# Turning x for the MLP's pairs 4 to 7 on VectorE instead of TensorE, in a fused transformer block

## The chip, the cores and the metric

The kernel runs on one core of a Trainium2 chip. A core has five engines, each with its own queue of instructions that it works through in order: TensorE (PE in the profile; PEld are its weight loads), VectorE (DVE), ScalarE (ACT), GpSimd (POOL) and SyncE (SP, which here only starts transfers). Engines wait for each other by semaphores. Transfers between the chip's DRAM and the on-chip memory (SBUF) run on 16 DMA engines, started from SP's, ACT's or POOL's queue. Matrix products land in PSUM, which ACT and DVE read.

The metric is the device time of one execution, in microseconds (us). The kernel before takes 766.53 us, the median of three runs (766.48 to 767.01).

## The reference

All is float32, for S = 2048 tokens, D = 640 features, 32 heads of 20, and F = 1728 hidden features:

```
mod = (silu(c) @ w_mod) in six rows of 640: sa, ca, ga, sb, cb, gb
h = layernorm(x) * (1 + ca) + sa
x = x + ga * linear_attention(h)              # softmax feature maps, then @ wo
h = layernorm(x) * (1 + cb) + sb              # layernorm over the 640 features of a token
r = relu(h @ w1 + b1)
x = x + gb * ((r * r) @ w2 + b2)
```

The change lies in the second layernorm and in how its result is brought to the MLP's first product.

## The kernel before

The attention half takes the first half of the time; its result for token tile t (128 tokens) lies in DRAM as `A1[t]`. The MLP then goes over eight **pairs** j = 0 to 7 of two token tiles, 256 tokens each. Float32 products are made of three products of rounded parts (high times high, high times low, low times high), so each operand exists as a high and a low part.

For a pair j the MLP runs seven **rounds** n = 0 to 6, and each round has two **steps**: step 2n and step 2n + 1, so that a pair has steps 0 to 13. In step s TensorE makes `up(j, s)`: 128 hidden features for the 256 tokens, 15 matmuls over the five blocks d of the features (10 in step 13, whose tile is half). ACT takes it from PSUM with bias and relu into `ft` (`ACTIVATE ft<-up`), DVE squares it there. After the second step of a round ACT copies the high parts into `ra`, DVE makes the low parts of it (`ra<-ft,ra`) and four sums (`ft<-ft` of 128 elements) that the next step splits into `rs` in the same way. From `ra` TensorE makes the first half of the down product, `down(0)`, in the following even step, behind `up`; from `rs` the second half, `down(1)`, in the following odd step. For pairs from 2 on, four of the operands of `down` come through rings of four buffers, fetched by POOL's queue (`t_fetch`), and a seven-product scheme replaces eight products.

The MLP reads the normalised input turned: features on the partitions, tokens along the row, in five blocks d = 0 to 4 (`H2[j]`, named `h` in the profile). While pair j is in work, the input of pair j + 1 is made ready in small pieces; `layer(j + 1, s)` puts a piece behind step s. The table `LN_AT` says at which step each piece stands (`LN_AT0`, `LN_AT1` and `LN_AT2` do it for pairs 1 to 3). The pieces are:

- `load`: `xm` gets `A1`'s two tiles, `xx` the block's input x (both token-major: tokens on the partitions).
- `add`: DVE adds `xx` to `xm`; SP stores the sum as `X1[j]`, which is read again later as the residual (`xr<-x`).
- `ln`: six pieces, two each of a sum, a sum of squares and a normalising pass over the 640 features (all ACT, with small work on POOL in between for mean, variance and the power -0.5).
- the entries 8, 10 and 12, which name blocks d: `t2` turns these blocks with TensorE (`t_in`, four transposes for two blocks, two for one), and `t_out` applies scale and shift by feature on ACT, makes the high part on ACT and the low part on DVE.

The result of pair j - 1 is finished in rounds 0 to 2 of pair j (`first_combos`, `end`, `gate`, `finish`), and `finish` also stores it to `out` through SP's queue.

The order within each engine's queue is that in which the code is written; from pair 2 on SP's queue is included.

Of the kernel before, what the change touches and what calls it, by code (L numbers as in the profile page):

```python
# [8 lines left out]
F32 = mybir.dt.float32  # L9
# [6 lines left out]
P = 128  # L16
S = 2048
D = 640
# [17 lines left out]
KEPT = NT - POSTPONED  # L36
W2_AT = 48
PLAIN = 2
DIRECT = 2
LAST = 3  # L40
W_AT = (
# [10 lines left out]
def kernel(  # L52
# [47 lines left out]
    tiny.tile([P, 144], F32, name="fill2")  # L100
# [16 lines left out]
    def row(tag, name):  # L117
        return (pc if tag in ("s3", "s4") else mem).tile([P, D], F32, tag=tag, name=name, bufs=BUFS[tag])
# [13 lines left out]
    def small(shape, tag, name, bufs=2):  # L132
        return (pc if tag in ("mx", "sk", "dn", "dd") else tiny).tile(shape, F32, tag=tag, name=name, bufs=bufs)
# [4 lines left out]
    def tp(name):  # L138
        return psA.tile([P, 512], F32, tag="tp", name=name)
# [160 lines left out]
    def mod_turn(part, p, *cs_):  # L300
        t = MT.setdefault(part, None) or row("s1", f"mt{part}")
        MT[part] = t
        a, n = cs_[0] * P, len(cs_) * P
        for i, c in enumerate(cs_):
            nc.tensor.transpose(p[:, i * P : (i + 1) * P], MA[part][:, c * P : (c + 1) * P], ident)
        nc.scalar.activation(t[:, a : a + n], p[:, :n], AF.Copy)

    def mod_sum(part, dest):
# [43 lines left out]
        for _ in ln_parts(xt, nm, spare):  # L352
            pass

    def t_in(xn, d, p):
        for i in range(2):
            nc.tensor.transpose(p[:, i * P : (i + 1) * P], xn[:, i, d * P : (d + 1) * P], ident)  # L357

    def t_unit(xn, cols, hT, d, nm, p=None):
        if p is None:  # L360
            p = tp(f"t{nm}_{d}")
        t_in(xn, d, p)
        t_out(cols, hT, d, nm, p)

    def t_out(cols, hT, d, nm, p, hf=None):
        if hf is None:
            hf = row("s3", f"hf{nm}_{d}")[:, :256]
        nc.scalar.activation(hf, p[:, :256], AF.Identity, bias=cols[:, d : d + 1], scale=cols[:, 5 + d : 6 + d])
        nc.scalar.activation(hT[:, d, 0], hf, AF.Copy)
        lo(hT[:, d, 1], hf, hT[:, d, 0])  # L370
# [723 lines left out]
    NB = NT // 2  # L1094
    places += [new(f"w{w}") for w in W_AT[-23:-19] + W_AT[-18:-16] + W_AT[-15:]] + [new(tag) for tag in ("k", "k", "q0", "q1")]
# [396 lines left out]
    LN_AT0 = {"load": 2, "xx": 3, "add": (5, 6), "ln": (5, 6, 7, 7, 8, 9), 10: (0, 1), 11: (2, 3), 12: (4,)}  # L1492
    LN_AT1 = {"load": 3, "add": (5, 5), "ln": (5, 6, 6, 7, 8, 8), 9: (0, 1), 11: (2, 3), 12: (4,)}
    LN_AT2 = {"load": 0, "xx": 3, "add": (6, 6), "ln": (7, 7, 8, 8, 9, 9), 10: (0, 1), 11: (2, 3), 12: (4,)}
    LN_AT = {"load": 0, "add": (3, 4), "ln": (4, 5, 6, 6, 7, 7), 8: (0, 1), 10: (2, 3), 12: (4,)}
    PREPS = iter([1, 3] + [2, 1, 2, 2, 1, 2] + [1, 1] + [1, 2])

    def ln_pieces(xt, nm, spare):
        sm = small([P, 2], "sm", f"sm{nm}")
        sq = small([P, 2], "sq", f"sq{nm}")  # L1500
        nb = small([P, 2], "nb", f"nb{nm}")
        for i in range(2):
            nc.scalar.activation(spare[i], xt[:, i], AF.Identity, accum_out=sm[:, i : i + 1])
            if i:
                nc.gpsimd.tensor_scalar(sm, sm, -1.0 / D, None, op0=ALU.mult)
            yield
        for i in range(2):
            nc.scalar.activation(spare[i], xt[:, i], AF.Square, bias=sm[:, i : i + 1], accum_out=sq[:, i : i + 1])
            if i:
                nc.gpsimd.tensor_scalar(sq, sq, 1.0 / D, EPS, op0=ALU.mult, op1=ALU.add)  # L1510
                nc.gpsimd.tensor_tensor(sq, sq, mhalf, op=ALU.pow)
                nc.gpsimd.tensor_tensor(nb, sm, sq, op=ALU.mult)
            yield
        for i in range(2):
            nc.scalar.activation(xt[:, i], xt[:, i], AF.Identity, bias=nb[:, i : i + 1], scale=sq[:, i : i + 1])
            yield

    def layer(j, at, part=None):
        todo = {1: LN_AT0, PLAIN: LN_AT1, PLAIN + 1: LN_AT2}.get(j, LN_AT)
        if j == NB:  # L1520
            return
        if part != 1:
            if at in todo:
                t2(j, *todo[at])
            if todo["load"] == at:
                load_xm(j)
            if todo.get("xx", todo["load"]) == at:
                load_xx(j)
            for i in range(2):
                if todo["add"][i] == at:  # L1530
                    add_x(j, i)
        if part == 0:
            return
        for i in range(6):
            if todo["ln"][i] == at:
                if i == 0:
                    LN2[j] = ln_pieces(XM[j], f"b{j}", XX[j])
                next(LN2[j])

    for j in range(NB):  # L1540
        if j <= PLAIN:
# [161 lines left out]
```

## Time and profile before

| what | us |
|---|---|
| median of three runs | 766.53 |
| the profiled execution | 766.05 |
| its span, from the first to the last instruction | 764.3 |
| TensorE busy in it | 758.5 |
| VectorE busy | 593.9 |
| ScalarE busy | 435.6 |
| GpSimd busy | 144.9 |

The granted TensorE clock was 1.000 of full speed over the whole span. The views used are the page (busy times, the chain that ended last, the costliest groups), the groups of instructions by line and shape, the table of busy times by stretch of time, and the timeline of an engine, where equal neighbours are merged: start, length, engine, line, operation, out<-in, shapes, count, and in square brackets the idle time of the engine before it. Matmuls overlap in the pipeline, so a matmul's own length says less than the distance between starts. All stretches below lie in pair 4's rounds, which begin at 573.63 us; there pair 5 is made ready. Its steps 6 to 12 begin at 592.90, 596.15, 599.40, 603.01, 606.40, 610.01 and 613.42 us.

### The profile page before, as it was taken

What the parts mean: (1) busy time and instruction counts of PE and PEld (TensorE: products, weight loads), DVE (VectorE), ACT (ScalarE), POOL (GpSimd) and SP (SyncE); (2) the same over time, 40 slices, a digit from 0 to 9 for tenths busy, and PEclk for the clock granted to TensorE, in tenths of its full rate; (3) what the DMA queues carried; (4) which work ended last, traced back from release to release, by engine and by line L of the source; (5) the groups of instructions that cost most, each with busy time, mean ns of one, the idle gap of its engine ahead of it and who ended that gap; (6) DMA issues with size and microseconds to landing.
All of it is one profiled execution on the core that took longest, in us unless ns stands there. A gap on an engine that the chain in (4) does not pass through costs nothing.

```text
span 764.3 us, 15303 instructions
## 1 busy us (share of the span) xinstructions
PE 758.5 (99%) x5968; PEld 739.7 (97%) x5968; DVE 593.9 (78%) x1083; ACT 435.6 (57%) x972; POOL 144.9 (19%) x301
## 2 busy tenths in 40 slices
PE   9999999999999999999999999999999999999997
PEld 8999999999999989988999999999999999999997
DVE  6598897988999899999655667876767666685666
ACT  5766756677853364546776647465563645536331
POOL 3001101001100255432101000231321313213110
PEclk9999999999999999999999999999999999999999
DMA  8811431343332345223366466996766759767460
GB/s 322 329 61 78 138 104 54 104 136 112 126 104 93 109 150 188 72 87 104 122 194 221 120 227 236 283 334 209 224 166 207 232 179 268 199 184 204 126 184 35
DMA packets 51505, 126.69 MB, mean 166 GB/s; under 512 B 6684, under 2 KB 7457, under 8 KB 51433
## 3 DMA queue, kind: packets, MB, share of 16 engines
q1 hardware_dynamic: 34098, 84.65, 32.8%
q0 software_dynamic: 14752, 35.76, 16.9%
q10 hardware_dynamic: 2583, 5.30, 1.8%
q8 instruction: 47, 0.77, 0.5%
q14 instruction: 25, 0.20, 0.1%
HBM read 95.70 MB, written 29.89 MB: 164 GB/s over the span
## 4 chain that ended last, share of the span: by engine, by line
PE 91%; DVE 7%; DMA 1%; issue 0%; SPq 0%; ACT 0%; DVEq 0%
PE up L78 24%; PE acc L78 18%; PE pq L78 9%; PE pk L78 9%; PE pv L78 9%; PE pwo L78 6%; PE acc3x L78 5%; PE kvp L450 3%; PE te L920 1%; DVE dn L878 1%; DVE scr L876 1%; DVE ezb L900 1%; PE tb L357 1%; PE ta L357 1%; DVE ot L88 1%; PE foldq L280 1%
## 5 line engine op out<-in xcount | busy, mean ns | idle before, releaser
L78 PE MATMUL up<-h,w 128*128 128x256 f32 x1640 | 206.4, 278 | 0.0
L78 PEld LDWEIGHTS up<-h,w 128*128 128x128 f32 x1640 | 196.1, 188 | 0.0
L1255 ACT ACTIVATE ft<-up,b_t 128x256 f32<-128x256 f32 x104 | 49.1, 472 | 113.8 <-PE up L78 113.2
L78 PE MATMUL acc<-w,ra 128*128 128x384 f32 x452 | 97.4, 335 | 0.0
L1256 DVE TENSOR_TENSOR ft<-ft 128x256 f32<-128x256 f32 x104 | 44.1, 424 | 48.4 <-ACT ft L1255 46.8
L78 PE MATMUL pwo<-wo,ot 128*128 128x256 f32 (+3 forms) x512 | 80.5, 312 | 0.1
L78 PEld LDWEIGHTS pwo<-wo,ot 128*128 128x128 f32 (+1 forms) x512 | 74.4, 188 | 3.2 <-issue 2.7
L78 PE MATMUL pq<-wq,hT 128*128 128x384 f32 (+1 forms) x480 | 75.2, 312 | 0.0
L78 PEld LDWEIGHTS acc<-w,ra 128*128 128x128 f32 x452 | 72.7, 188 | 0.8 <-DVE ra L88 0.5
L78 PE MATMUL pk<-wk,hT 128*128 128x384 f32 (+1 forms) x480 | 72.7, 308 | 0.0
L78 PE MATMUL pv<-wv,hT 128*128 128x384 f32 (+1 forms) x480 | 71.7, 307 | 0.0
L78 PEld LDWEIGHTS pq<-wq,hT 128*128 128x128 f32 x480 | 71.1, 188 | 0.6 <-issue 0.2
L78 PEld LDWEIGHTS pk<-wk,hT 128*128 128x128 f32 x480 | 70.5, 188 | 0.4 <-issue 0.2
L78 PEld LDWEIGHTS pv<-wv,hT 128*128 128x128 f32 x480 | 70.1, 188 | 0.0
L88 DVE TENSOR_TENSOR ra<-ft,ra 128x384 fp32r<-128x384 f32 (+2 forms) x86 | 36.8, 449 | 32.6 <-ACT ra L1279 19.3
L1365 POOL DMA_DIRECT2D ring_a<-td_a x34 | 18.3, 539 | 126.1 <-PE acc L78 100.4
L1279 ACT ACTIVATE ra<-ft 128x384 fp32r<-128x384 f32 x48 | 25.2, 526 | 28.4 <-DVE ft L1256 22.4
L78 PE MATMUL acc3x<-w,ra 128*128 128x256 f32 x231 | 39.8, 278 | 0.0
L78 PEld LDWEIGHTS acc3x<-w,ra 128*128 128x128 f32 x231 | 37.2, 188 | 0.2 <-DVE ra L88 0.2
L1270 DVE TENSOR_TENSOR ft<-ft 128x128 f32<-128x128 f32 x136 | 33.4, 287 | 1.2
L441 DVE TENSOR_REDUCE sk<-ek 128x64 f32<-128x1280 f32 x16 | 23.7, 1484 | 12.4 <-ACT ek L436 10.8
L884 POOL TENSOR_TENSOR dn<-dn,rs_q 128x32 f32<-128x32 f32 x32 | 20.2, 630 | 66.7 <-DVE dn L878 66.4
(270 smaller groups left out, 1412.6 us busy)
## 6 DMA issues: line engine op xcount, KB each, us to landing
ring_c<-td_c POOLq DMA_DIRECT2D x34, 384.0 KB, 4.2
ring_a<-td_a POOLq DMA_DIRECT2D x34, 384.0 KB, 4.1
ring_b<-td_b POOLq DMA_DIRECT2D x34, 256.0 KB, 4.0
esp<-eq SPq DMA_DIRECT2D x12, 640.0 KB, 3.0
el<-esp SPq DMA_DIRECT2D x12, 640.0 KB, 3.9
rw<-in_w SPq DMA_DIRECT2D x23, 320.0 KB, 2.9
wm<-in_w_mod SPq DMA_DIRECT2D x20, 320.0 KB, 3.3
xb<-in_x SPq DMA_DIRECT2D x8, 640.0 KB, 4.2
```

The costliest lines, as they stand in the source:

```text
L78: nc.tensor.matmul(o, a, b, start=first and i == 0, stop=last and i == len(terms) - 1, skip_group_check=skip,)
L88: (eng or nc.vector).tensor_tensor(out_lo, full, hi.bitcast(F32), op=ALU.subtract)
L280: nc.tensor.matmul(p[g // 3][:, (g % 3) * 120 : (g % 3) * 120 + n], r, bd_t[:120, g * 120 : g * 120 + n], start=True, stop=True,)
L357: nc.tensor.transpose(p[:, i * P : (i + 1) * P], xn[:, i, d * P : (d + 1) * P], ident)
L441: nc.vector.tensor_reduce(s, heads(flat(e)), axis=AX.X, op=ALU.add)
L450: nc.tensor.matmul(kvp[g // 4][64 * c : 64 * c + 64, a : a + 2 * n].rearrange("p (s n) -> p s n", s=2), v[:, u], e[:, :, o : o + n], start ...
L884: nc.gpsimd.tensor_tensor(dn[:, s], dn[:, s], rs[:, 1 - s], op=ALU.mult)
L1255: nc.scalar.activation(r, p, AF.Relu, bias=b1_t[:, f : f + 1])
L1256: nc.vector.tensor_tensor(r, r, r, op=ALU.mult)
L1270: nc.vector.tensor_tensor(t[:, o], t[:, a], t[:, b], op=op)
L1279: nc.scalar.activation(a[:, 0, :3], t[:, :3], AF.Copy)
L1365: nc.gpsimd.dma_start(RING[j, n, r], TD[n][r].bitcast(F32R))
```

## The change

For the pairs 4 to 7 (`j >= DEALT`) TensorE no longer turns the input. Instead:

- After the sum is stored to `X1[j]`, eight transfers on SP's queue (`load_dealt`) bring the raw sum back into `xx` by quarters of the features: partition 32q + t holds, for the four groups a of 32 tokens, the 160 features of quarter q of token 32a + t. They stand ahead of the store of the second half of the previous pair's result.
- The sums for the layernorm are made as before from `xm`, with one scratch row `junk` in place of `xx`, and each one or two steps earlier.
- Scale and shift by token (`rn`, two numbers for each of two tiles) are copied into `rna` for the new layout: 16 copies of 32 partitions by 4 numbers, eight on ACT and eight on DVE, in step 6.
- The normalising pass runs on `xx`, 160 elements at a time with the scale of its group: four passes in step 7 and four in step 8 in place of two of 640 in step 7.
- DVE turns `xx` in blocks of 32 by 32 into `xm` (`turn`, one instruction for each half of the pair, in steps 8 and 9). It reads with a step of five elements: block b holds the features 5k + b.
- `t_out` reads `xm` from SBUF in place of PSUM and works in place, for blocks 0 and 1 in step 10, 2 and 3 in step 11, and 4 in step 12.

Since features now are dealt over the blocks as 5k + b everywhere, w1's rows are packed so on the host, and the transposes that stay on TensorE (pairs 0 to 3, and the two rows of `mod` that give scale and shift) read their 128 columns with a step of five elements, that is 20 bytes.

```diff
-            nc.tensor.transpose(p[:, i * P : (i + 1) * P], MA[part][:, c * P : (c + 1) * P], ident)
+            src = by_turn(MA[part])[:, c] if part in (3, 4) else MA[part][:, c * P : (c + 1) * P]
+            nc.tensor.transpose(p[:, i * P : (i + 1) * P], src, ident)
...
-        p = tp(f"tb{j}_{ds[0]}")
-        for k, d in enumerate(ds):
-            t_in(XM[j], d, p[:, 256 * k : 256 * k + 256])
+        if j >= DEALT:
+            for d in ds:
+                hf = XM[j].rearrange("p s d -> p (s d)")[:, 256 * d : 256 * d + 256]
+                t_out(cols_b, H2[j], d, f"b{j}", hf, hf)
+            return
+        p = tp(f"tb{j}_{ds[0]}")
+        for k, d in enumerate(ds):
+            t_in(XM[j], d, p[:, 256 * k : 256 * k + 256], True)
...
+    def by_turn(ap):
+        return ap.rearrange("p (f b) -> p b f", b=NC)
+
+    def t_in(xn, d, p, mixed=False):
         for i in range(2):
-            nc.tensor.transpose(p[:, i * P : (i + 1) * P], xn[:, i, d * P : (d + 1) * P], ident)
+            src = by_turn(xn[:, i])[:, d] if mixed else xn[:, i, d * P : (d + 1) * P]
+            nc.tensor.transpose(p[:, i * P : (i + 1) * P], src, ident)
...
+    def load_dealt(j):
+        for i in range(2):
+            for q in range(4):
+                nc.sync.dma_start(
+                    XX[j][i][32 * q : 32 * q + 32].rearrange("t (a c) -> t a c", a=4),
+                    X1[j][:, i, 160 * q : 160 * q + 160].rearrange("(a t) c -> t a c", a=4),
+                )
+
+    def turn(j, i):
+        xt = XM[j].rearrange("p s d -> p (s d)").rearrange("p (b i a t) -> p i a b t", b=NC, i=2, t=32)
+        nc.vector.transpose(xt[:, i], XX[j][i].rearrange("p (a t b) -> p a b t", a=4, t=32))
...
-    LN_AT = {"load": 0, "add": (3, 4), "ln": (4, 5, 6, 6, 7, 7), 8: (0, 1), 10: (2, 3), 12: (4,)}
+    LN_AT = {"load": 0, "add": (3, 3), "dealt": 4, "ln": (4, 4, 5, 5, 6, 7, 8), "turn": (8, 9), 10: (0, 1), 11: (2, 3), 12: (4,)}
...
+    def ln_dealt(j):
...
+        for a in range(4):
+            for q in range(4):
+                o, v = ra[32 * q : 32 * q + 32, a], rn[32 * a : 32 * a + 32]
+                if q % 2:
+                    nc.scalar.activation(o, v, AF.Copy)
+                else:
+                    nc.vector.tensor_copy(o, v)
+        yield
+        for i in range(2):
+            for a in range(4):
+                x = XX[j][i][:, 160 * a : 160 * a + 160]
+                nc.scalar.activation(x, x, AF.Identity, bias=ra[:, a, i, 1:2], scale=ra[:, a, i, 0:1])
+            yield
...
-    w1 = np.stack([np.tile(w, (1, P // w.shape[1])).reshape(NC, P, P).transpose(1, 0, 2) for w in w1])
+    w1 = np.stack([np.tile(w, (1, P // w.shape[1])).reshape(P, NC, P) for w in w1])
```

How the order moves is shown for pair 4's rounds, where pair 5 is made ready. In TensorE's queue, steps 8 and 9 of the kernel before (`acc...ring_c` ends `down(0)`, `tb` are the transposes, `acc...ring_a` begins `down(1)`):

```order
L78 MATMUL up<-h_4_6999,w_8_4803 128x256 x15
L78 MATMUL acc_4_7312<-w_6_4898,ra_3_7515 128x384 x3
L78 MATMUL acc_4_7316<-w_7_4943,ra_3_7515 128x384 x3
L78 MATMUL acc_4_7320<-ring_3_c,ra_3_7515 128x384 x3
L357 MATMUL tb_0_7573<-ident,xm_7238 128x128 x4
L78 MATMUL up<-h_4_6999,w_9_4861 128x256 x15
L78 MATMUL acc_4_7353<-ring_3_a,rs_3_7558 128x384 x3
```

and after:

```order
L79 MATMUL up<-h_4_7106,w_8_4803 128x256 x15
L79 MATMUL acc_4_7332<-w_6_4898,ra_3_7560 128x384 x3
L79 MATMUL acc_4_7336<-w_7_4943,ra_3_7560 128x384 x3
L79 MATMUL acc_4_7340<-ring_3_c,ra_3_7560 128x384 x3
L79 MATMUL up<-h_4_7106,w_9_4861 128x256 x15
L79 MATMUL acc_4_7373<-ring_3_a,rs_3_7605 128x384 x3
```

The row with `tb` is gone here and in steps 10 and 12, for each of the pairs 5 to 7, and for pair 4 in pair 3's rounds; the other rows stand as they were.

In VectorE's queue, from the sums of step 9 to the square of step 11, before (`xr` is the residual with its bias, `h` the low part of the turned input):

```order
L1270 TENSOR_TENSOR ft_4_7555<-ft_4_7555 128x128 x4
L1256 TENSOR_TENSOR ft_5_7639<-ft_5_7639 128x2x128
L88 TENSOR_TENSOR rs_4_7642<-ft_4_7555,rs_4_7642 128x512
L1424 TENSOR_TENSOR xr_4_0_7494<-xr_4_0_7494,bb 128x640
L1424 TENSOR_TENSOR xr_4_1_7496<-xr_4_1_7496,bb 128x640
L88 TENSOR_TENSOR h_5_7572<-xx_0_7241,h_5_7572 128x256
L88 TENSOR_TENSOR h_5_7572<-xx_1_7242,h_5_7572 128x256
L1256 TENSOR_TENSOR ft_5_7639<-ft_5_7639 128x256
```

and after:

```order
L1293 TENSOR_TENSOR ft_4_7602<-ft_4_7602 128x128 x4
L1115 STREAM_TRANSPOSE xm_7258<-xx_1_7262 128x4x5x32
L1279 TENSOR_TENSOR ft_5_7680<-ft_5_7680 128x2x128
L89 TENSOR_TENSOR rs_4_7683<-ft_4_7602,rs_4_7683 128x512
L1447 TENSOR_TENSOR xr_4_0_7539<-xr_4_0_7539,bb 128x640
L1447 TENSOR_TENSOR xr_4_1_7541<-xr_4_1_7541,bb 128x640
L89 TENSOR_TENSOR h_5_7699<-xm_7258,h_5_7699 128x256 x2
L1279 TENSOR_TENSOR ft_5_7680<-ft_5_7680 128x256
```

The turning of the second half has come in between the sums and the square of step 10, ahead of all that follows in this queue.

In ScalarE's queue, steps 6 to 8 before (`rs` and `ra` with one input are the high parts):

```order
L1255 ACTIVATE ft_3_7472<-up,b_t 128x2x128
L1295 ACTIVATE rs_2_7475<-ft_2_7389 128x512
L1508 ACTIVATE xx_0_7241,sqb_7409<-xm_7238,smb_7408 128x640
L1508 ACTIVATE xx_1_7242,sqb_7409<-xm_7238,smb_7408 128x640
L1255 ACTIVATE ft_3_7472<-up,b_t 128x256
L1279 ACTIVATE ra_3_7515<-ft_3_7472 128x384
L1515 ACTIVATE xm_7238<-xm_7238,nbb_7410,sqb_7409 128x640 x2
L1255 ACTIVATE ft_4_7555<-up,b_t 128x2x128
L1295 ACTIVATE rs_3_7558<-ft_3_7472 128x512
```

and after:

```order
L1278 ACTIVATE ft_3_7506<-up,b_t 128x2x128
L1318 ACTIVATE rs_2_7509<-ft_2_7411 128x512
L1563 ACTIVATE rna_7430<-rn_7429 32x4 x8
L1278 ACTIVATE ft_3_7506<-up,b_t 128x256
L1302 ACTIVATE ra_3_7560<-ft_3_7506 128x384
L1570 ACTIVATE xx_0_7261<-xx_0_7261,rna_7430 128x160 x4
L1278 ACTIVATE ft_4_7602<-up,b_t 128x2x128
L1318 ACTIVATE rs_3_7605<-ft_3_7506 128x512
L1570 ACTIVATE xx_1_7262<-xx_1_7262,rna_7430 128x160 x4
```

The sums of squares have moved from step 6 to step 5, the eight small copies took their place, and the passes of 160 stand in steps 7 and 8, where they wait for the eight transfers.

More of the change, by code (lines that the diff above doesn't have):

```diff
@@ L38 @@
 PLAIN = 2
+DEALT = 4
 DIRECT = 2
@@ L99 @@
     tiny = ctx.enter_context(tc.tile_pool(name="tiny", bufs=1))
-    tiny.tile([P, 144], F32, name="fill2")
+    tiny.tile([P, 120], F32, name="fill2")
     p12 = ExitStack()
@@ L353, in layer_norm @@
             pass
-    def t_in(xn, d, p):
+    def by_turn(ap):
+        return ap.rearrange("p (f b) -> p b f", b=NC)
+    def t_in(xn, d, p, mixed=False):
         for i in range(2):
-            nc.tensor.transpose(p[:, i * P : (i + 1) * P], xn[:, i, d * P : (d + 1) * P], ident)
+            src = by_turn(xn[:, i])[:, d] if mixed else xn[:, i, d * P : (d + 1) * P]
+            nc.tensor.transpose(p[:, i * P : (i + 1) * P], src, ident)
     def t_unit(xn, cols, hT, d, nm, p=None):
@@ L361, in t_unit @@
             p = tp(f"t{nm}_{d}")
-        t_in(xn, d, p)
+        t_in(xn, d, p, True)
         t_out(cols, hT, d, nm, p)
@@ L1533, in layer @@
             return
-        for i in range(6):
-            if todo["ln"][i] == at:
+        for i in range(2):
+            if j >= DEALT and todo["turn"][i] == at:
+                turn(j, i)
+        for i, k in enumerate(todo["ln"]):
+            if k == at:
                 if i == 0:
-                    LN2[j] = ln_pieces(XM[j], f"b{j}", XX[j])
+                    LN2[j] = ln_dealt(j) if j >= DEALT else ln_pieces(XM[j], f"b{j}", XX[j])
                 next(LN2[j])
+        if todo.get("dealt") == at:
+            load_dealt(j)
     for j in range(NB):
```

17 lines of the change are left out of this document (added).

## The prediction

> **What bounds the kernel now.** I read the page first, for the busy times and the chain of work that ended last:
>
> ```profile
> PE 758.5 (99%) x5968; PEld 739.7 (97%) x5968; DVE 593.9 (78%) x1083; ACT 435.6 (57%) x972; POOL 144.9 (19%) x301
> ...
> PE 91%; DVE 7%; DMA 1%; issue 0%; SPq 0%; ACT 0%; DVEq 0%
> ```
>
> TensorE carries 91% of the chain. A busy PE need not be at its peak, so next comes the table of busy times by stretch; each row is one round of pair 4, from the start of its first `up` to that of the next round's:
>
> ```profile
> core 0: us, PE busy (x) PEld busy (x) DVE busy (x) ACT busy (x) POOL busy (x), PEclk, DMA share, GB/s
> ...
> 586.40:592.90 6.50, 6.50 (x54) 6.50 (x52) 5.21 (x11) 2.71 (x7) 1.60 (x4) 1.00 0.78 234
> 592.90:599.40 6.50, 6.50 (x54) 6.50 (x52) 3.74 (x9) 4.34 (x11) 3.00 (x8) 1.00 1.01 318
> 599.40:606.40 7.00, 7.00 (x58) 6.96 (x56) 3.79 (x10) 5.33 (x11) 1.95 (x4) 1.00 0.78 226
> 606.40:613.42 7.02, 7.02 (x57) 6.99 (x56) 5.17 (x12) 3.76 (x9) 1.60 (x4) 1.00 0.55 152
> 613.42:619.60 6.18, 6.18 (x50) 6.14 (x49) 3.80 (x11) 3.14 (x8) 1.58 (x4) 1.00 0.61 156
> sum 45.97, PE 45.97 PEld 45.87 DVE 31.00 ACT 23.59 POOL 11.31; mean PE 6.57 PEld 6.55 DVE 4.43 ACT 3.37 POOL 1.62
> ```
>
> Rounds with the same work take 6.50 us to the hundredth, whatever DVE and ACT do beside them (3.74 to 5.21 us and 2.71 to 4.34 us busy), and the two rounds with four transposes take 0.50 and 0.52 us more. So these rounds are bound by TensorE's own instructions, and what is taken out of its queue is time gained, as long as nothing else becomes late. DVE has 15 us free in a pair, ACT 22 us; the question is only at which places.
>
> **What is removed.** For each of four pairs ten transposes leave TensorE. Their own length (first row, from the view of this tile: 270, 272 and 310 ns as least, median and most) is not their price, since they overlap; the price is read from the distance between starts in TensorE's timeline:
>
> ```profile
> L357 PE MATMUL tb<-ident,xm x80: 270/272/310, 381.8 to 708.7; 128*128 128x128 f32 x80
> ...
> 596.15 1.87 PE L78 MATMUL up<-h,w 128*128 128x256 f32 x15
> 597.86 0.68 PE L78 MATMUL acc<-ring_a,rs 128*128 128x384 f32 x3
> ...
> 602.65 0.60 PE L357 MATMUL tb<-ident,xm 128*128 128x128 f32 x4
> 603.01 2.01 PE L78 MATMUL up<-h,w 128*128 128x256 f32 x15
> 604.86 0.68 PE L78 MATMUL acc<-ring_a,rs 128*128 128x384 f32 x3
> ...
> 616.68 0.38 PE L357 MATMUL tb<-ident,xm 128*128 128x128 f32 x2
> 616.82 1.41 PE L78 MATMUL up<-h,w 128*128 128x256 f32 x10
> 618.06 0.68 PE L78 MATMUL acc<-ring_a,rs 128*128 128x384 f32 x3
> ```
>
> Fifteen matmuls of `up` take 1.71 us (596.15 to 597.86). With four transposes ahead: 0.36 us until `up` starts, and `up` takes 1.85 us, 0.14 more: 0.50. With two ahead: 0.14, and ten matmuls take 1.24 instead of 1.14: 0.24. A pair: 0.50 + 0.52 + 0.24 = 1.26 us; four pairs: 5.0 us, or 0.126 us for a transpose. [...]
>
> **What is added on TensorE.** The 40 transposes of pairs 0 to 3, and ten of `mod`'s two rows, load their data with a step of 20 bytes. No row shows such a load, but the groups by shape show how loads of a transpose grow with their columns (count, then busy us and mean ns):
>
> ```profile
> L920 PEld LDWEIGHTS te<-ident,ezb 128*120 128x120 f32 x160 | 17.9, 137 | 0.6 <-ACT ept L922 0.3
> L920 PEld LDWEIGHTS te<-ident,ezb 128*80 128x80 f32 x16 | 1.8, 119 | 0.2
> L1190 PEld LDWEIGHTS gbt<-ident,gate_b 128*5 128x5 f32 x1 | 0.1, 88 | 0.0
> ```
>
> From 5 to 120 columns a load grows by 49 ns, 0.43 ns a column, so 128 columns take about 55 ns beyond a fixed part. A transpose costs 0.126 us, which leaves 70 ns of cover for the next load. Twice as slow a column is covered: 0. Four times as slow is 3 x 55 = 165 ns more, 95 uncovered, times 50: 4.7 us. Below zero it cannot go, as nothing is taken away. I take 0, since nothing in the trace says a step costs more than double, and keep 4.7 us for the range.
>
> **ScalarE, steps 6 to 8 and 11.** The sums and squares are as many as before. The eight copies of 4 numbers, the narrow passes and what they displace are priced from one group of small copies and from ACT's and POOL's timelines:
>
> ```profile
> L421 ACT ACTIVATE vt<-pv 128x24 f32<-128x24 f32 x16 | 3.0, 185 | 0.0
> ...
> 594.86 0.48 ACT L1255 ACTIVATE ft<-up,b_t 128x256 f32<-128x256 f32 x1 [1.08 <-PE up L78]
> ...
> 598.06 0.48 ACT L1255 ACTIVATE ft<-up,b_t 128x256 f32<-128x256 f32 x1 [0.58 <-PE up L78]
> 599.03 0.53 ACT L1279 ACTIVATE ra<-ft 128x384 fp32r<-128x384 f32 x1 [0.49 <-DVE ft L1256]
> 599.46 1.73 ACT L1515 ACTIVATE xm<-xm,nbb,sqb 128x640 f32<-128x640 f32 x2
> 601.30 0.48 ACT L1255 ACTIVATE ft<-up,b_t 128x256 f32<-128x256 f32 x1
> ...
> 597.57 0.18 POOL L1510 TENSOR_SCALAR sqb<-sqb 128x2 f32<-128x2 f32 x1 [0.27 <-ACT xx L1508]
> ...
> 598.63 0.41 POOL L1512 TENSOR_TENSOR nbb<-smb,sqb 128x2 f32<-128x2 f32 x1
> ```
>
> Step 6: POOL's variance work lasts 1.47 us (597.57 to 599.04). The squares now stand in step 5, where two of them (0.9 us each) fit into the time that one sum and 1.08 us of idleness leave ahead of step 6's `ft` (594.86), so POOL is done at 596.4, and eight copies of 0.19 end at 597.9, just ahead of step 7's `ft` (598.06). Step 7: a pass of 640 lasts 0.87 (1.73 for two); by the widths of ACT's rows (24 elements 185 ns, 640 some 900) a pass of 160 takes about 0.35 to 0.5 us, so four take 1.4 to 2.0 in place of 1.73: step 8's `ft` is on time or 0.2 us late. Behind it stand the two parts of `rs`, which TensorE wants at 604.86, 3.5 us after that `ft` starts (3.0 without the transposes): covered. Step 11 gets two blocks of `t_out` (four passes, 2 us) like the 1.73 us here. The fits of steps 6 and 11 are within 0.2 us, so I allow 0.1 us for each pair, 0.4 in all; ends 0 and 0.5 each.
>
> **VectorE: the turn.** The two turns of 640 elements in each pair are the largest unknown; the nearest groups are a pass over as many elements and one over twice as many, and the tightest place is round 5 in DVE's timeline:
>
> ```profile
> L1079 DVE TENSOR_TENSOR xm<-xm,xx 128x640 f32<-128x640 f32 x16 | 12.8, 819 | 0.0
> L878 DVE TENSOR_REDUCE dn<-scr 128x64 f32<-128x1280 f32 x16 | 23.8, 1486 | 0.6
> ...
> 607.10 1.02 DVE L1270 TENSOR_TENSOR ft<-ft 128x128 f32<-128x128 f32 x4
> 608.80 0.43 DVE L1256 TENSOR_TENSOR ft<-ft 128x256 f32<-128x256 f32 x1 [0.69 <-ACT ft L1255]
> ...
> 612.25 0.43 DVE L88 TENSOR_TENSOR h<-xx,h 128x256 fp32r<-128x256 f32 x1 [0.42 <-ACT h L369]
> 612.61 0.42 DVE L1256 TENSOR_TENSOR ft<-ft 128x256 f32<-128x256 f32 x1
> 613.63 0.56 DVE L88 TENSOR_TENSOR ra<-ft,ra 128x384 fp32r<-128x384 f32 x1 [0.59 <-ACT ra L1279]
> ```
>
> So a turn takes 0.82 to 1.49 us; I take about 1, near the pass of the same width. The first stands in step 8, where the low parts of `h` no longer do (they move to steps 10 and 11). The second stands behind the sums of step 9. Up to the square at 612.61 DVE is idle 0.69 + 0.42 us and some tenths between instructions, 1.2 us in all, of which 0.5 goes because TensorE comes earlier without the transposes: 0.7. From the square the chain runs to `ra` at 614.19, and TensorE needs that at the end of the next `up`, 1.71 us behind the round's start at 613.42: 615.13, so 0.9 more. A turn of up to 1.6 us costs nothing, and both bounds lie below. The eight copies on DVE (step 6, of 4 numbers each) fall into a round in which DVE is busy 3.74 of 6.50 us. Two adds instead of one in step 3 delay step 4's square by one pass, 0.8 us, and take it from behind that square; the round has DVE free for 1.29 us (5.21 of 6.50), so I take it as covered.
>
> **SP and the transfers.** SP's queue has the store of the sum, then eight loads that wait for it, then the previous result's store. Its timeline, and the page's list of transfers with KB and median us to landing:
>
> ```profile
> 588.84 2.32 SPq L1080 DMA_DIRECT2D x<-xm  x2
> 595.37 0.34 SPq L1421 DMA_DIRECT2D out<-y  x1
> ...
> xx<-in_x SPq DMA_DIRECT2D x16, 320.0 KB, 5.0
> x<-xm SPq DMA_DIRECT2D x16, 320.0 KB, 3.0
> ```
>
> Both stores can now start by 589.7 and land by 592.7. Eight issues of about 0.4 us run until 596, in quarters of 80 KB. With 5.0 us to landing, as loads of four times the size take here, the first half is there by 598.9 and the second by 601; step 7's passes want the first at 599.5, step 8's the second at 602.2. Covered by 0.6 us or more: 0. The store of the result, queued behind, starts up to 1 us later than at 595.37; only SP waits there. The next pair's `xm` load waits for the last low part of `h` instead of the last transpose, about 1 us later, and its add stands three steps, 10 us, behind.
>
> **The sum.** -5.0 (transposes) + 0 (loads with a step) + 0.4 (ScalarE's tight fits) + 0 (turn) + 0 (transfers) = -4.6 us against the profiled execution's 766.05: 761.4. The median of the runs is 0.48 above that execution, so the forecast for a median is **761.9 us**, 0.6% faster; its own range is 761.2 to 764.
>
> **Rivals.**
> - *Loads with a step cost TensorE what the removed ones gain.* At four times a column's time 4.7 us of the 5.0 are gone: 766.53 - 5.0 + 4.7 + 0.4 = 766.6, no change. [...]
> - *The turn is so slow that DVE becomes late (the other side).* Place: steps 9 to 11. Beyond 1.6 us each further us delays `rs` and `ra` by as much, once a pair. From 1.6 + 1.26 = 2.9 us on the kernel is slower; at 4 us it is 4 x (2.4 - 1.26) = 4.6 us slower: 771. For it: no row shows such an instruction, nor a read with this step; against it: it would need more than three times the time of a pass of that width.
> - *The eight loads land late.* ACT stands at step 7 until they are there, and with it all `ft`. Late by 2 us more than its slack (landing about 8 us after issue), the gain shrinks by 1 to 1.5 us a pair: 766.5 to 767.5. For it: 640-byte pieces, and DMA busy at 1.01 in that round; against it: quarters of the size.
> - *Nothing is gained, as TensorE would wait there anyway.* 766.5. Against it: 6.50 us in each round without transposes.
>
> **Chances.** Forecast 0.72, slow loads 0.11, slow turn 0.07, late transfers 0.06, no gain 0.04. What the measurement can tell from no change is about 0.2%, 1.5 us. Faster by more: 0.72, 0.06 of the slow loads (partial cost) and 0.02 of the late transfers, 0.80; within: 0.03 of the slow loads, 0.02 of the transfers and 0.04, 0.09; slower: the rest, 0.11. The range reaches from the full 5.0 with 0.3 of scatter, 761.2, up into slow loads at most of their price, 765.8.
>
> **What would show it.** Rounds 3 and 4 of the pairs 3 to 6 take 6.50 us and the next 5.94 instead of 7.00, 7.02 and 6.18: right. TensorE's loads of the pairs 1 to 3 stay near 140 ns and four transposes at 0.50 us: no step penalty. The turn's row says its length, idle time on TensorE before `acc` with `ra` or `rs` in rounds 5 and 6 that it is too long, and an ACT wait for `xx<-x` at its passes that the loads are late. A turn above 2.9 us, or 0.2 us per remaining transpose, makes the forecast wrong.

## The result, and the profile after

The changed kernel takes 761.71 us (median of six runs, 760.99 to 762.71) against 766.50 us for the kernel before beside it: a ratio of 0.9936, with a 95% interval from 0.9923 to 0.9949. The profiled execution takes 761.45 us, with a span of 759.7 instead of 764.3 us, so 4.6 us less.

The page of the changed kernel, busy times and chain:

```profile
PE 754.3 (99%) x5928; PEld 736.3 (97%) x5928; DVE 607.0 (80%) x1123; ACT 449.0 (59%) x1028; POOL 145.0 (19%) x301
...
PE 92%; DVE 7%; issue 0%; ACT 0%; POOL 0%; DVEq 0%; POOLq 0%
```

TensorE has 40 instructions fewer and is 4.2 us less busy; VectorE and ScalarE are 13 us busier each, and TensorE still carries the chain. The table of busy times by stretch, with one row for each round of pair 4 from steps 4 and 5 on (span, then PE, PEld, DVE, ACT and POOL busy, granted clock, DMA share, GB/s):

```profile
585.49:591.99 6.50, 6.50 (x54) 6.50 (x52) 5.02 (x11) 3.54 (x9) 1.86 (x5) 1.00 0.93 295
591.99:598.49 6.50, 6.50 (x54) 6.50 (x52) 5.09 (x17) 5.01 (x17) 3.18 (x7) 1.00 1.09 267
598.49:604.99 6.50, 6.50 (x54) 6.50 (x52) 4.25 (x9) 5.51 (x13) 1.60 (x4) 1.00 0.98 327
604.99:611.49 6.50, 6.50 (x54) 6.50 (x52) 6.13 (x13) 3.67 (x9) 1.58 (x4) 1.00 0.65 163
611.49:617.42 5.93, 5.93 (x48) 5.93 (x47) 4.50 (x13) 5.00 (x12) 1.58 (x4) 1.00 0.60 139
```

The three rounds of 7.00, 7.02 and 6.18 us are now 6.50, 6.50 and 5.93: 1.27 us a pair. VectorE is busy 6.13 of 6.50 us in the round of the second turn, so hardly anything is left there. What the added work costs for itself, from the groups by shape and from the groups of the tiles `tb` (count, busy us and mean ns; for `tb`: least, median and most ns):

```profile
L1115 DVE STREAM_TRANSPOSE xm<-xx 128x640 f32<-128x640 f32 x8 | 10.9, 1359 | 0.0
L1565 DVE COPY rna<-rn 32x4 f32<-32x4 f32 x32 | 5.4, 170 | 0.8
...
L1563 ACT ACTIVATE rna<-rn 32x4 f32<-32x4 f32 x32 | 6.5, 203 | 3.8 <-POOL rn L1557 3.3
L1570 ACT ACTIVATE xx<-xx,rna 128x160 f32<-128x160 f32 x32 | 14.0, 509 | 0.0
...
L363 PEld LDWEIGHTS tb<-ident,xm x40: 191/202/218, 381.5 to 525.1; 128*128 128x128 f32 x40
```

A turn takes 1.36 us, a copy 0.20 us on ScalarE and 0.17 on VectorE, a narrow pass 0.51. The loads with a step of 20 bytes take 202 ns where they took 140.

Along the span, by the starts of TensorE's steps: the four pairs 3 to 6, in which pairs 4 to 7 are made ready, each gain 1.27 us (5.1 in all). Against it stand 0.34 us in steps 10 to 13 of pair 2 (the expectations below call them 0.36), where pair 3 is made ready and the transposes are still there, and a pause of 0.13 us in step 9 of pair 5. That gives the 4.6 us. The pause is a wait for a ring's fetch, as POOL's timeline, the fetch's time to landing and the timeline of weight loads show:

```profile
640.75 0.62 POOL L1388 DMA_DIRECT2D ring_a<-td_a  x1 [0.37 <-issue]
...
DMA to landing us min/median/max: 7.3/7.3/7.3
...
648.17 0.47 PEld L79 LDWEIGHTS acc<-ring_a,rs 128*128 128x128 f32 x3
```

and the time to landing of the same fetch in the kernel before:

```profile
DMA to landing us min/median/max: 5.3/5.3/5.3
```

The fetch takes 7.3 us and lands at 648.06, and the first weight load for the product that reads it starts 0.11 us later. In the four pairs this fetch takes 5.3 to 5.7 us before and lands at least 2.3 us before it is wanted; now it takes 5.6 to 7.3 us, and 0.1 to 1.7 us are left.

The experiments ask where the 0.34 us come from, what the added work costs, and how near it stands to costing something.

### The profile page after: what moved, and what is told of

Same layout as the page of the kernel before. It is cut to its first block, busy times and chain, and to the rows that moved or that the text cites. A ratio compares the mean times of both kernels' runs of the same rounds, so it can differ in the third digit from the quotient of the medians.

```text
span 759.7 us, 15397 instructions
## 1 busy us (share of the span) xinstructions
PE 754.3 (99%) x5928; PEld 736.3 (97%) x5928; DVE 607.0 (80%) x1123; ACT 449.0 (59%) x1028; POOL 145.0 (19%) x301
## 4 chain that ended last, share of the span: by engine, by line
PE 92%; DVE 7%; issue 0%; ACT 0%; POOL 0%; DVEq 0%; POOLq 0%
PE up L79 25%; PE acc L79 18%; PE pq L79 9%; PE pk L79 9%; PE pv L79 9%; PE pwo L79 6%; PE acc3x L79 5%; PE kvp L456 3%; PE te L926 1%; DVE dn L884 1%; DVE scr L882 1%; DVE ezb L906 1%; PE foldk L281 1%; PE ta L363 1%; DVE ot L89 1%; PE foldq L281 1%
```

## The experiments

Ratios are to the kernel before, run beside each on the same chip; the changed kernel stands at 0.9936. One thousandth is 0.77 us.

| run | ratio | 95% interval | against the changed kernel, us |
|---|---|---|---|
| straight | 0.9938 | 0.9924 to 0.9951 | +0.2 |
| before_step | 1.0013 | 1.0004 to 1.0022 | (to before: +1.0) |
| bare | 1.0019 | 1.0011 to 1.0028 | +6.4 |
| bare2 | 0.9928 | 0.9911 to 0.9944 | -0.6 |
| fill_kept | 1.0013 | 1.0002 to 1.0023 | +5.9 |
| fill_128 | 1.0056 | 1.0039 to 1.0073 | +9.2 |
| fill_184 | 0.9949 | 0.9934 to 0.9964 | +1.0 |
| before_120 | 1.0068 | 1.0053 to 1.0083 | (to before: +5.2) |
| turn_twice | 0.9987 | 0.9978 to 0.9996 | +3.9 |
| copies_act | 1.0018 | 1.0009 to 1.0027 | +6.3 |
| loads_later | 1.0094 | 1.0073 to 1.0114 | +12.1 |
| pair3 | 1.0043 | 1.0030 to 1.0057 | +8.2 |

### Loads with a step: taken away, and alone

After the result I laid these 0.34 us of pair 2 to the longer loads. The first run takes the step away:

```diff
-        t_in(xn, d, p, True)
+        t_in(xn, d, p)
...
-            src = by_turn(MA[part])[:, c] if part in (3, 4) else MA[part][:, c * P : (c + 1) * P]
+            src = MA[part][:, c * P : (c + 1) * P]
...
-            t_in(XM[j], d, p[:, 256 * k : 256 * k + 256], True)
+            t_in(XM[j], d, p[:, 256 * k : 256 * k + 256])
```

> The changed kernel, but the 50 transposes that stay on TensorE (pairs 0 to 3, scale and shift) read their columns side by side again; the features of these pairs then do not fit w1's packing, so the values are not the block's, the work is the same. Theory (loads with a step take about 60 ns longer, which a group of four transposes cannot cover; pair 3's preparation lost 0.36 us by it, the others nothing): 0.3 to 0.4 us less than the changed kernel, pair 3's three groups back at 3.81, 3.70 and 3.52 us, loads back at 140 ns. Rival, the forecast's term (a load twice as slow is covered): no difference, and the 0.36 us have another cause.

The second gives the step to the kernel before, for all its transposes of the MLP:

```diff
-            nc.tensor.transpose(p[:, i * P : (i + 1) * P], xn[:, i, d * P : (d + 1) * P], ident)
+            src = by_turn(xn[:, i])[:, d] if mixed else xn[:, i, d * P : (d + 1) * P]
+            nc.tensor.transpose(p[:, i * P : (i + 1) * P], src, ident)
...
-            t_in(XM[j], d, p[:, 256 * k : 256 * k + 256])
+            t_in(XM[j], d, p[:, 256 * k : 256 * k + 256], True)
...
-    w1 = np.stack([np.tile(w, (1, P // w.shape[1])).reshape(NC, P, P).transpose(1, 0, 2) for w in w1])
+    w1 = np.stack([np.tile(w, (1, P // w.shape[1])).reshape(P, NC, P) for w in w1])
```

> The kernel before with one part of the change alone: all its 80 transposes of the MLP and ten of scale and shift load with a step of 20 bytes, w1 packed to fit, nothing else. Theory (load 60 ns longer, 0.36 us lost in each pair whose preparation TensorE bounds, pairs 3 to 7): 1.8 us slower than before, 0.2%; rounds with four transposes 7.15 to 7.2 us in place of 7.00. Rival by the forecast's cover of 70 ns: no difference. Rival by four times a column's time, 95 ns uncovered for each of 50 transposes: 4.8 us slower.

The loads of `tb` in `straight`, and in `before_step` pair 4's three rounds that hold the transposes:

```profile
L363 PEld LDWEIGHTS tb<-ident,xm x40: 138/141/143, 381.8 to 525.4; 128*128 128x128 f32 x40
```

```profile
599.71:606.74 7.03, 7.03 (x57) 7.03 (x56) 3.79 (x10) 5.34 (x11) 1.96 (x4) 1.00 0.77 234
606.74:613.74 7.00, 7.00 (x57) 7.00 (x56) 5.17 (x12) 3.72 (x9) 1.59 (x4) 1.00 0.59 152
613.74:619.97 6.23, 6.23 (x51) 6.23 (x49) 3.83 (x11) 3.18 (x8) 1.61 (x4) 1.00 0.64 165
```

The theory of 0.36 us a pair falls. With the step the three rounds take 7.03, 7.00 and 6.23 us, without it 7.00, 7.02 and 6.18: 0.06 us a pair, where the theory wanted 0.36 and four times a column's time 0.95. The load is 60 ns longer, and 6 ns of it for each transpose are seen in the steps: the rest is covered, as the forecast had it. (The last rival counts 50 transposes; in this kernel 90 load with a step, so four times a column's time would have cost 8.6 us. The median of this run is 1.0 us above before, 0.3 to 1.7; the two profiled spans differ by 0.4. The steps show no place for more.)

What pair 2 does lose is seen in the timeline of weight loads, before and then after; the wait stands in brackets:

```profile
516.67 0.48 PEld L78 LDWEIGHTS acc<-ring_c,ra 128*128 128x128 f32 x3 [0.24 <-DMA ring_c<-td_c]
```

```profile
516.86 0.47 PEld L79 LDWEIGHTS acc<-ring_c,ra 128*128 128x128 f32 x3 [0.33 <-DMA ring_c<-td_c]
```

TensorE waits there for a ring's transfer, in the kernel before too. In `straight` the same wait lies one step earlier and takes 0.66 us, in `bare2` and `before_step` there is none, in `copies_act` it is 1.56. It differs from run to run, each of which has one trace here; that it makes a part of the scatter between executions is likely, but not shown. Where it is absent or lies outside, steps 10 to 13 of pair 2 can be compared with and without a step, in `bare2` and then in `straight`:

```profile
513.61:527.40 13.79, 13.79 (x110) 13.79 (x108) 9.66 (x25) 10.23 (x22) 3.54 (x7) 1.00 0.66 196
```

```profile
514.65:528.28 13.63, 13.63 (x109) 13.56 (x108) 8.98 (x24) 9.49 (x21) 3.10 (x6) 1.00 0.68 190
```

So 0.16 of the 0.34 us are the loads with a step, and the other 0.18 lie in the step with the ring's wait.

### The added work taken away, and the place of the buffers

The run `bare` leaves out the eight loads, the copies and the turn, and the buffer `rna` with them (the core of the edit):

```diff
-    ra = tiny.tile([P, 4, 2, 2], F32, tag="rna", name=f"rna{j}", bufs=1)
...
-        if todo.get("dealt") == at:
-            load_dealt(j)
```

> The changed kernel without what it adds for the turn: no eight loads, no 16 copies of the factors, no turn on VectorE (the values are then not the block's); the narrow passes and the rest stay. Theory (the added work lies wholly beside TensorE's): within 0.2 us of the changed kernel. Rival, the forecast's term for ScalarE's tight fits: 0.4 us faster than the changed kernel, and more if the turn of 1.36 us or the loads cost something unseen.

It came out 6.4 us *slower* than the changed kernel, with less work. TensorE waits for nothing in the pairs 3 to 6; its rounds are longer everywhere in the MLP (6.60 us against 6.50 in the rows below), also in pair 0, where nothing was left out. The one thing that differs there is where the buffers lie: `rna` takes 64 bytes in each partition, and all that is allocated behind it had moved. Here is a line of the change that I had not priced at all: ahead of the small buffers stands a filler, and the change cuts it from 144 numbers to 120 (576 to 480 bytes), while it adds `rn` and `rna`. `bare2` is `bare` with those 64 bytes filled again:

```diff
-    tiny.tile([P, 120], F32, name="fill2")
+    tiny.tile([P, 136], F32, name="fill2")
```

> As the run without eight loads, copies and turn (the values are not the block's), but the 64 bytes that the factors' missing buffer freed are filled again, so that every later buffer lies where it lies in the changed kernel. Theory (that run was slower in every step of the MLP, 6.58 us a round in place of 6.50, by the place of its operands in memory, not by the missing work): rounds of 6.50 us and the time of the changed kernel, 761.7 within 0.4. Rival by ScalarE's tight fits: 761.3. Rival (the missing work itself makes TensorE slower): 768 again.

`fill_kept` is the whole change without the cut of the filler:

```diff
-    tiny.tile([P, 120], F32, name="fill2")
+    tiny.tile([P, 144], F32, name="fill2")
```

> The changed kernel with the filler ahead of the small buffers left at 144 numbers in place of 120, so that everything behind it lies 96 bytes further on than in both kernels. Theory of the place: TensorE's rounds get longer than 6.50 us all through the MLP, by up to the 0.08 us of the 64-byte shift, so up to 6 us slower than the changed kernel. Rival (the place is not the cause, or only that shift is): 761.7.

The round of steps 6 and 7 of pair 4, in `bare`, in `bare2` and in `fill_kept`:

```profile
589.55:596.16 6.61, 6.61 (x54) 6.61 (x52) 5.03 (x11) 3.54 (x9) 1.82 (x5) 1.00 0.92 299
596.16:602.76 6.60, 6.60 (x53) 6.60 (x52) 3.74 (x9) 3.73 (x9) 3.25 (x7) 1.00 0.87 246
```

```profile
584.87:591.37 6.50, 6.50 (x54) 6.50 (x53) 5.03 (x11) 3.54 (x9) 1.87 (x5) 1.00 0.92 284
591.37:597.87 6.50, 6.50 (x54) 6.50 (x53) 3.73 (x9) 3.71 (x9) 3.17 (x7) 1.00 0.86 253
```

```profile
595.48:602.10 6.62, 6.62 (x54) 6.62 (x53) 5.10 (x17) 5.07 (x17) 3.25 (x7) 1.00 1.14 257
```

(In `bare` and `bare2` the row ahead, steps 4 and 5, stands with it.) With the 64 bytes back the rounds are 6.50 us. The medians, 0.9928 against 0.9936, have intervals too wide to tell 0.4 us; the pairs tell it. Pairs 3 to 6 take 44.70 us each in `bare2`, and 44.70, 44.70, 44.83 and 44.70 in the changed kernel. Pair 5, in `bare2` and then in the changed kernel:

```profile
616.80:661.50 44.70, 44.70 (x354) 44.70 (x352) 30.64 (x77) 25.41 (x57) 11.40 (x23) 1.00 0.73 215
...
617.42:662.25 44.83, 44.83 (x354) 44.77 (x353) 34.32 (x87) 26.95 (x65) 11.41 (x23) 1.00 0.79 230
```

So the copies and turns lie wholly beside TensorE's work, and the 0.4 us for ScalarE's tight fits are not there. What the added work can cost is the wait for `ring_a` in step 9, 0.13 us here. Waits of this kind, 0.1 to 0.75 us, each ending 0.1 us behind the landing of `ring_a`, stand in pairs 3 to 6 of `straight`, `fill_kept`, `fill_128`, `fill_184`, `turn_twice` and `pair3` too, and in no run without the eight loads. That points to the loads, which run beside the fetch (DMA share of the round of steps 6 and 7: 0.86 in `bare2`, 1.09 in the changed kernel); no run changes them alone.

With the filler left as it was, the same change is 5.9 us slower than the changed kernel, and with 1.0013 (1.0002 to 1.0023) nothing is left of the gain over before: it hangs on the cut of the filler.

Two more fillers, and the kernel before with the shorter filler alone, tell how the place counts:

```diff
-    tiny.tile([P, 120], F32, name="fill2")
+    tiny.tile([P, 128], F32, name="fill2")
```

> The changed kernel with the filler at 128 numbers, everything behind it 32 bytes further on. Shifts of 64 bytes to the front and of 96 further on cost 6.4 and 6.3 us. If the place is the best of its neighbourhood, 2 to 7 us slower than the changed kernel; if 32 bytes are below what matters, 761.7; if the place was never the best, it can also be faster.

```diff
-    tiny.tile([P, 120], F32, name="fill2")
+    tiny.tile([P, 184], F32, name="fill2")
```

> The changed kernel with the filler at 184 numbers, everything behind it 256 bytes further on. If the place counts only within a period of 256 bytes or a part of it, 761.7 as the changed kernel; if it counts by more address bits, slower by up to 7 us, or another value.

```diff
-    tiny.tile([P, 144], F32, name="fill2")
+    tiny.tile([P, 120], F32, name="fill2")
```

> The kernel before with one line of the change alone, the filler of 120 numbers in place of 144, so that everything behind it lies 96 bytes further to the front. Theory of the place (the change's new small buffers take just these 96 bytes, the filler keeps all others where they were, and another place makes TensorE's products slower): several us slower than before, as the changed kernel with the old filler was by 6.3. Rival (only the changed kernel is sensitive to it): 766.5.

The same round (steps 6 and 7 of pair 4) in `fill_128` and `fill_184`, and steps 4 and 5 in `before_120`:

```profile
597.47:604.14 6.67, 6.67 (x54) 6.67 (x52) 5.10 (x17) 5.10 (x17) 3.27 (x7) 1.00 1.07 289
```

```profile
592.75:599.25 6.50, 6.50 (x53) 6.50 (x52) 5.09 (x17) 5.00 (x17) 3.17 (x7) 1.00 1.09 259
```

```profile
588.83:595.44 6.61, 6.61 (x53) 6.61 (x52) 5.21 (x11) 2.72 (x7) 1.59 (x4) 1.00 0.85 230
```

A shift of 32 bytes costs most (6.67 us a round, 9.2 us in all), one of 64 to the front 6.4, one of 96 further on 5.9; one of 256 bytes leaves the rounds at 6.50, and its 1.0 us in the median is within the intervals. (Waits for a ring in pair 2, 0.99 us in `fill_128` and 1.12 in `fill_184`, are in the profiled executions of both.) The kernel before is sensitive in the same way: 96 bytes to the front cost it 5.2 us. The granted clock is 1.00 in all these rows, and TensorE waits for nothing in them. What grows is the distance between matmuls: in the pairs from 560 us on, two matmuls of `up` start 113.4 ns apart on average in the changed kernel, 114.2 in `fill_kept`, 115.6 in `bare`, 116.7 in `fill_128`. Which pairs of operands must not lie how was not found out; a period of 256 or of 128 bytes fits all of them.

### A longer turn

The turn's length cannot be chosen, but the second one can be done twice:

```diff
             if j >= DEALT and todo["turn"][i] == at:
-                turn(j, i)
+                for _ in range(2 if i else 1):
+                    turn(j, i)
```

> The changed kernel with the second turn of each pair (step 9) done twice, so 1.36 us more on VectorE at its tightest place, four times. By the forecast (free up to 1.6 us, from there a us for a us): 2.72 - 1.6 = 1.1 us a pair, 4.5 us slower than the changed kernel. By the timeline of the changed kernel (rs has 1.09 us until TensorE wants it, ra 0.7): 1.36 - 0.7 = 0.65 us a pair, 2.6 us slower. Rival (VectorE catches up elsewhere, the slack is larger): no difference.

3.9 us slower: 1.0 us a pair for 1.36 us more on VectorE. So 0.4 us of the second turn were free. If each further us costs a us, which one length cannot show, a turn of up to 1.36 + 0.4, some 1.7 us, is free (an estimate), where the forecast had 1.6. The path is another than the forecast's, though. ScalarE's and TensorE's weight-load timelines of pair 4, steps 10 to 13:

```profile
610.39 0.60 ACT L374 ACTIVATE xm<-xm,cols_b 128x256 f32<-128x256 f32 x1 [1.45 <-DVE xm L1115]
...
612.30 0.46 ACT L1278 ACTIVATE ft<-up,b_t 128x256 f32<-128x256 f32 x1
```

```profile
611.32 0.19 PEld L79 LDWEIGHTS acc<-ring_a,rs 128*128 128x128 f32 x1 [0.18 <-DVE rs L89]
...
612.80 1.79 PEld L79 LDWEIGHTS up<-h,w 128*128 128x128 f32 x15 [0.19 <-ACT ft L1278]
...
616.60 0.54 PEld L79 LDWEIGHTS up<-h,w 128*128 128x128 f32 x4 [0.49 <-ACT ft L1278]
```

`rs` comes 0.18 us late, as the forecast's chain says, and `ra` 0.12 us, which is too short for the timeline to mark it. The larger part, 0.19 and 0.49 us, comes through ScalarE: its `t_out` waits 1.45 us for the turn, the next `ft` stands behind four passes of it in ScalarE's queue, and TensorE's next `up` waits for `ft`, since the products of the next step may only be written when ScalarE has read the last ones.

### ScalarE's copies

If TensorE's `up` waits for the `ft` before it, ScalarE's step 6 must be a tight place: after the copies `ft` starts at 597.48 and the next `up` is due at 598.49. All 16 copies on ScalarE:

```diff
-                if q % 2:
-                    nc.scalar.activation(o, v, AF.Copy)
-                else:
-                    nc.vector.tensor_copy(o, v)
+                nc.scalar.activation(o, v, AF.Copy)
```

> The changed kernel with all 16 copies of the factors on ScalarE, none on VectorE: 8 more at 0.22 us, 1.74 us more ahead of step 7's ft, which starts at 597.48 in pair 4. By the forecast's reading (a late ft counts only through rs and ra, with about 3 us of cover for rs): no difference to a few tenths. By the wait that the late loads showed (TensorE's next up waits for the ft of the last, as they share one buffer): ft done at 599.7 where the next up is due at 598.49, 1.2 us a pair, 4.8 us slower than the changed kernel, with TensorE's up waiting for ft in step 8 and no drop of the clock for pauses that short.

ScalarE and TensorE in pair 4, steps 7 and 8:

```profile
599.05 3.46 ACT L1562 ACTIVATE rna<-rn 32x4 f32<-32x4 f32 x16 [0.82 <-POOL rn L1557]
602.54 0.47 ACT L1278 ACTIVATE ft<-up,b_t 128x256 f32<-128x256 f32 x1
```

```profile
601.49 0.50 PE L79 MATMUL acc<-ring_b,rs 128*128 128x256 f32 x3
603.06 1.99 PE L79 MATMUL up<-h,w 128*128 128x256 f32 x15 [1.07 <-ACT ft L1278]
```

TensorE idles 1.07 us at just this place; the two steps take 1.35 us more than in the changed kernel, 5.3 us over the four pairs (1.22 to 1.36 each). In this execution the ring's wait of pair 2, 1.56 us, comes on top. The reading that a late `ft` counts only through `rs`, three us later, is refuted: a `ft` has about half a us to spare, and the split of the copies over two engines is needed.

### The loads behind the result's store

```diff
-    LN_AT = {"load": 0, "add": (3, 3), "dealt": 4, "ln": (4, 4, 5, 5, 6, 7, 8), ...
+    LN_AT = {"load": 0, "add": (3, 3), "dealt": 5, "ln": (4, 4, 5, 5, 6, 7, 8), ...
```

> The changed kernel with the eight loads one step later, so that they stand behind the store of the previous result in SP's queue, which waits for VectorE's last add at 594.4 us. Theory (0.6 us of slack in the forecast, ScalarE stands at step 7's passes with step 8's ft behind them): issue from 594.8, first half landed about 601 in place of 599, ft 2.5 us late, rs 1.2 us late for TensorE: 1.2 to 1.5 us a pair, 5 to 6 us slower than the changed kernel. Rival (transfers are hidden there as well): 761.7.

12.1 us slower, twice what was expected. SP, ScalarE and TensorE in pair 4, whose step 8 begins here at 602.20 (598.49 in the changed kernel), and the stretches of steps 8 and 9:

```profile
598.18 0.34 SPq L1444 DMA_DIRECT2D out<-y  x1
598.62 3.83 SPq L1108 DMA_DIRECT2D xx<-x  x8
```

```profile
605.94 1.75 ACT L1570 ACTIVATE xx<-xx,rna 128x160 f32<-128x160 f32 x4 [3.25 <-DMA xx<-x]
607.60 0.46 ACT L1278 ACTIVATE ft<-up,b_t 128x256 f32<-128x256 f32 x1
```

```profile
604.94 0.68 PE L79 MATMUL acc<-ring_c,ra 128*128 128x384 f32 x3
608.11 3.45 PE L79 MATMUL up<-h,w 128*128 128x256 f32 x15 [2.48 <-ACT ft L1278]
```

```profile
602.20:608.11 5.91, 3.43 (x27) 3.11 (x25) 1.48 (x6) 2.66 (x7) 1.15 (x3) 1.00 1.14 303
608.11:613.07 4.96, 4.96 (x27) 4.96 (x28) 2.77 (x4) 3.10 (x7) 0.47 (x1) 0.66 0.36 128
```

The loads are issued where expected: 3.6 us ahead of step 8, against 7.9 us in the changed kernel. ScalarE then waits 3.25 us for the first four quarters, `ft` is late, and TensorE idles 2.48 us. Then comes what was not expected: the granted clock in the next step is 0.66 on average, and its fifteen matmuls take 3.45 us instead of 1.87. In finer stretches the clock is 0.50 for 3.41 us and 1.00 behind them, here and in pair 6, where the pause was 2.16 us:

```profile
608.27:611.68 3.41, 3.41 (x17) 3.41 (x18) 2.19 (x3) 2.04 (x6) 0.00 (x0) 0.50 0.48 170
...
703.84:707.25 3.41, 3.36 (x15) 3.36 (x16) 2.38 (x3) 2.17 (x5) 0.00 (x0) 0.50 0.65 234
```

Pair 4 so loses 4.4 us; the four lose 2.9, 4.4, 2.2 and 4.0. In pairs 3 and 5 TensorE's longest pauses were 1.71 and 1.60 us, and the clock stayed at 1.00. So the lower clock followed pauses of 2.16 and 2.48 us here, and did not follow those of 1.07 (in `copies_act`) to 1.71. What decides it, the length of a pause or when it falls, no run tells.

### Pair 3 as well

```diff
-DEALT = 4
+DEALT = 3
...
-    LN_AT2 = {"load": 0, "xx": 3, "add": (6, 6), "ln": (7, 7, 8, 8, 9, 9), 10: (0, 1), 11: (2, 3), 12: (4,)}
+    LN_AT2 = {"load": 0, "xx": 3, "add": (5, 5), "dealt": 6, "ln": (6, 6, 7, 7, 8, 9, 9), "turn": (10, 10), 11: (0, 1), 12: (2, 3), 13: (4,)}
```

> The change extended to pair 3, whose input is made ready in pair 2: sums from step 6, eight loads in step 6, turns in step 10, blocks in steps 11 to 13. Theory (0.126 us for each transpose that leaves TensorE's queue): the four steps that hold them, 13.82 us before, go to 12.44, so 1.3 us faster than the changed kernel, about 760.4. Rival (the pieces stand so late in pair 2 that ScalarE or VectorE hold up TensorE at its end): no gain, or up to 2 us slower.

8.2 us slower, four times the rival's worst. In the profiled execution 8.0 us lie in pair 2, and 1.1 in pair 3, nearly all in its step 0, where `up` waits for the late `h`. SP and ScalarE in pair 2, and the stretches of steps 10 and of 11 and 12:

```profile
505.58 1.75 SPq L1086 DMA_DIRECT2D x<-xm  x2
511.86 4.91 SPq L1108 DMA_DIRECT2D xx<-x  x8
```

```profile
519.80 1.75 ACT L1570 ACTIVATE xx<-xx,rna 128x160 f32<-128x160 f32 x4 [4.25 <-DMA xx<-x]
```

```profile
515.33:525.12 9.79, 3.52 (x27) 3.20 (x25) 1.48 (x6) 4.15 (x11) 1.06 (x2) 0.87 0.92 234
525.12:533.83 8.71, 8.71 (x52) 8.71 (x52) 6.98 (x14) 4.65 (x10) 1.06 (x2) 0.75 0.26 66
```

The stores of the sum are issued at 505.58, the loads can start only at 511.86, and ScalarE waits 4.25 us for them; TensorE idles 6.3 us, and the clock falls (0.87 and 0.75 on average in the two stretches). It is the mechanism of `loads_later`, not a full engine. In pair 2 the DMA engines are busy all the time just ahead of this place (share 1.02 and 1.03 in the two rounds from 501.52), which fits stores that take 6 us from issue to the first load; that this is the cause was not tried. None of the runs gives a whole kernel that beats the changed one.

## Why the prediction was right

**The transposes, -5.0.** Right: 5.1 us, and rounds of 6.50, 6.50 and 5.93 us as forecast (n = 4, 5 and 6; the prediction calls the first two rounds 3 and 4). The price by the distance between starts holds.

**Loads with a step, 0.** Right in the cover and nearly in the sum: the load takes 60 ns more, about the 55 that twice as slow a column would give, and it costs 0.06 us for ten transposes in the rounds of `before_step`, 0.16 in pair 2. No run shows four times a column's time, the source of the 4.7 us in the range: that would have made the load 165 ns longer, by the forecast's own estimate. My second thought, 0.36, was wrong.

**ScalarE's tight fits, +0.4.** Mis-sized: nothing is lost there (`bare2`). The sum came out on the profiled time all the same, because 0.34 us in pair 2 (half a ring's wait, half loads) and a wait of 0.13 us for another fetch, which the forecast did not have, stand in their place. The errors cancel, and the agreement to the tenth is chance. (The prediction names two upper ends of its range, 764 and 765.8 us; the result lies below both.)

**The turn, 0.** Right: 1.36 us lies in the upper half of the bounds, not near the 1 us taken, and is free. The limit of 1.6 us came out at some 1.7, by the estimate above.

**The transfers, 0.** Right for the order as it is: no pass of ScalarE waits for the loads. The term looks only at these loads, though; that a fetch of `ring_a` beside them lands late, 0.13 us here, it does not have. The rival's price was far off: late loads were to cost 1 to 1.5 us a pair, and loads that start 4.3 us later against step 8, for which ScalarE waits 2.4 to 3.3 us, cost 2.2 to 4.4. The step that failed is the sentence that behind step 8's `ft` only `rs` and `ra` wait: TensorE's next `up` waits for `ft` itself, and after pauses of 2.16 and 2.48 us the clock is lower (0.50 for 3.41 us).

**The rivals.** Loads with a step, a slow turn and no gain are excluded by `before_step`, the row of the turn and the rounds. Late loads is the one that is near: one step later in the table turns the gain into a loss.

**What the forecast did not see.** It argued from queues alone. The filler of 144 or 120 numbers stood in the change, and with it unaltered the forecast would have been wrong by nearly 6 us (`fill_kept`: 1.0013 of before, 767.5 us), with no gain over before.

## What to carry to other kernels

Where one engine bounds a stage, read what a change takes from its queue by the distance between starts (here 0.13 us a transpose, with a length of 0.27), and ask of the added work whether the engine's buffers still come back in time: here the copies and turns lay beside TensorE's work, 44.70 us for each of four pairs without them and for three of the four with them. Look first for the reader that frees the buffer the bound engine writes next; its slack was about half a us here, shorter than that of the data which comes later. When a buffer is added to or removed from a tuned kernel, keep the addresses of all others, and test an experiment that leaves out work with its buffers still in place: `bare`, with less work, was 6.4 us slower because its operands had moved by 64 bytes. A pause of TensorE can cost more than its length: in `loads_later` pair 4 lost 4.4 us with a pause of 2.48. Look at the landing of the fetches beside added transfers too: here a fetch took 5.6 to 7.3 us to landing beside the eight loads, 5.3 to 5.7 before.

## What was not expected of the hardware

- Moving the buffers by 32 to 96 bytes changes the distance between matmuls of 256 columns by 1 to 3% (113.4 ns on average, 114.2 to 116.7), at a clock of 1.00 and without a wait, and the kernel by 5 to 9 us; 256 bytes change nothing in the rounds. The mechanism is open.
- After pauses of 2.16 and 2.48 us of TensorE the granted clock was 0.50 for 3.41 us; after pauses of 1.07 to 1.71 us it stayed at 1.00.
- A weight load of a transpose with its elements 20 bytes apart takes 202 ns instead of 140, for 128 columns.
- The turn of 128 x 640 numbers in blocks of 32 by 32, read with a step of 20 bytes, takes 1.36 us on VectorE, where a sum over as many elements takes 0.82. Whether the step or the operation makes the difference was not tried.
